# Mamba-2 scan and cosine router on one core: sums of weights, a data-dependent loop and its tables moved in the order of the work

## The chip, the cores and the metric

The kernel runs on one NeuronCore of a Trainium2 chip. The metric is the time in microseconds (us) that the device takes for one launch; the time before is 300.6 us, the median of three runs (297.8 to 301.43). The core has five engines that each work through a queue of their own, in order: TensorE (PE: matmuls; PEld is its weight load), VectorE (DVE), ScalarE (ACT), GpSimd (POOL) and SyncE (SP, which here only starts DMAs). They meet through semaphores. Matmuls read from the on-chip memory SBUF and write sums to another, PSUM.

## The reference

A Mamba-2 scan makes 3072 tokens of 256 features, and a router with 8 experts turns each token into its output:

```
for c in range(nc):                               # scan in chunks
    y[:, :, sl] = (CB * L) @ xc + (Cc @ state) * exp(cum)
    state = decay_full * state + sum_j B_j x_j * decay_from_j
x = y.transpose(0, 2, 1, 3).reshape(3072, 256)
logits = normed(x) @ normed(expert_emb).T / tau
expert_idx = argmax(logits); gate = softmax(logits)[expert_idx]
for e in range(8):
    mask = expert_idx == e
    out[mask] = gate[mask, None] * (relu(x[mask] @ w1[e]) @ w2[e])
```

w1 is 8 x 256 x 1024, w2 is 8 x 1024 x 256, all in float32.

## The kernel before, in words

**The scan** (`mamba`) computes the tokens chunk by chunk, finds each token's expert, and scatters each token's row into a table `rows` in DRAM, sorted by expert. It ends at about 97 us of the profiled execution. **The experts** (`moe`) then run over that table. Room is made for 416 tokens of each expert (4 tiles of 104). What an expert has beyond that, "leftover" tokens, would be computed by a loop whose length is only known when the kernel runs; with these inputs its length is zero, and the loop's body is skipped by a branch.

The work is a list `parts` of ten, run in order:

- parts 0 and 1: the early **halves** (2 tiles) of experts 0 and 1, whose tokens come from the first chunks; part 0's upward product is still in the scan, its downward product opens the experts;
- parts 2 and 3: the late halves of experts 0 and 1;
- parts 4 to 9: the **whole experts** 2 to 7 (4 tiles each), of the class `Seven`.

A half (class `Job`) is an upward product `up` (eight groups of hidden features, L745, the relu alternately on ACT and on DVE), then `turn_x` (transposes of the next part's tokens on PE, L723), `turn_copies`, `prepare` (DVE, L703 to L714: it makes the rows to write to, `to`, and each token's `gate`; its square root is a `pow` on POOL, L696, and its exponential is on ACT, L710), and a downward product `down` (L762), whose two results ACT and DVE copy to `yoT` (L767, L769). The finished tokens of a part are turned, scaled and written during the next part's `up`, in `out`: transposes on PE (L778), a scaling `yo` on DVE or ACT in turn (L781, L783; four buffers), then on POOL a memset of `tick` (L784) and an indirect DMA (L785).

A whole expert uses Strassen-like products with seven instead of eight block products. It needs sums of weights, which POOL makes ahead of time: `mix_up` makes `m1` from w1 and `mix_down` makes `m2` from w2, four instructions each (L806, 128 x 512 float32). Each of `m1` and `m2` has two buffers. It also needs differences of the tokens, `dx`, four subtractions on DVE (`mix_x`, L825) at the end of the part ahead of it.

**The order.** Nothing is scheduled by a planner: `manual_schedule` keeps each engine's queue in the order in which the program issues instructions. The helper `part(i)` issues part i and then what prepares the parts after it. In the kernel before, the sums for part 4 are issued at the start of part 2 (`mix_up`) and of part 3 (`mix_down`), the sums for part i + 2 are issued at the end of part i from part 3 on, and behind a whole expert's products stands a copy of one number of its `gate` to `tick` on POOL (L965), ahead of the sums: POOL waits there until DVE has finished that part's `prepare`. Parts 1 to 3 have no such copy.

`leftover_blocks` (L1004 to L1059) computes the loop's tables in 23 small DVE instructions; it is issued at the end of part 1. `leftover` (L1062) stands between parts 7 and 8. It loads the number of blocks into a register of every engine (L1066) and branches on it (L1067). Where the body is skipped, each engine raises the semaphores by what the body would have raised; on POOL that includes the semaphores of its indirect DMAs (INC_SWDGE_SEM).

DMAs on SP: `begin(i + 3)` loads the tokens `xg` of a later part (two buffers), `load_weights` the weights of an expert (three buffers).

Of the kernel before, what the change touches and what calls it, by code (L numbers as in the profile page):

```python
# [28 lines left out]
EE, EC, HT = 2, 4, 2  # L29
# [173 lines left out]
def load_weights(k, e):  # L203
    k.w1t[e] = k.wp.tile([128, KD, F], F32, name="w1", tag="w1")
    k.nc.sync.dma_start(k.w1t[e][:], k.w1[e].rearrange("(k p) f -> p k f", p=128))
    k.w2t[e] = k.wp.tile([128, KF, DM], F32, name="w2", tag="w2")
    k.nc.sync.dma_start(k.w2t[e][:], k.w2[e].rearrange("(f p) m -> p f m", p=128))
# [721 lines left out]
def moe(k):  # L929
    parts = [(j, k.early_has[:TR, e, :]) for e, j in enumerate(k.early)]  # L930
    for e in range(EE):
        parts.append((Job(k, HT, TR, k.w1t[e], k.w2t[e]), k.late_has[:TR, e, :]))
    n = E + EE

    def begin(i):
        e = i - EE
        if e < EE:
            parts[i][0].load(k.p.tile([TR, HT, W], F32, name="xg", tag="xg"), T * e + HT * TR)
        else:
            parts.append((Seven(k, NT, TR, k.w1t[e], k.w2t[e]), k.has[:TR, e - EE, :]))  # L940
            parts[i][0].load(k.p.tile([TR, NT, W], F32, name="xg", tag="xg"), T * e)

    def part(i):
        j, has = parts[i]
        last, new = parts[i - 1][0], parts[i + 1][0] if i + 1 < n else None
        new_seven = isinstance(new, Seven)

        def out(at):
            if 0 <= at and 2 * at < last.nt:
                last.out(2 * at, 2)  # L950

        def turn():
            if new:
                new.turn_copies(k.nc.scalar.copy if new_seven else None)
            if new_seven:
                new.mix_x()

        if isinstance(j, Seven):
            for f in range(KF // 2):
                j.up(f)  # L960
                out(f)
            j.up(KF // 2, new.turn_x if new else None)
            j.mix_h()
            j.down(turn, lambda: j.prepare(has))
            k.nc.gpsimd.tensor_copy(out=k.tick[:], in_=j.gate[0:1, 0:1])  # L965
        else:
            if i == EE:
                parts[2 * EE][0].mix_up()
            elif new_seven:
                new.mix_down()  # L970
            for f in range(KF):
                j.up(f)
                out(f - 1)
                if f == 3:
                    j.measure()
            new.turn_x()
            turn()
            j.prepare(has)
            j.down(0, j.nt)
        if 2 * EE < i + 2 < n:  # L980
            parts[i + 2][0].mix_up()
            parts[i + 2][0].mix_down()
        if i == 1:
            leftover_blocks(k)
        if 0 <= i - EE < E - 3:
            load_weights(k, i - EE + 3)
        if i + 3 < n:
            begin(i + 3)

    with k.tc.manual_schedule():  # L990
        begin(EE)
        begin(EE + 1)
        parts[1][0].turn_x()
        parts[1][0].turn_copies()
        parts[0][0].down(0, HT)
        for i in range(1, n - 2):
            part(i)
        leftover(k)
        for i in range(n - 2, n):
            part(i)  # L1000
        parts[n - 1][0].out(0, NT)


def leftover_blocks(k):  # L1004


    nc = k.nc

    def tile_(name, shape, dtype=F32):
        return k.p.tile(shape, dtype, name=name, bufs=1)  # L1010

    def tt(out, in0, in1, op):
        nc.vector.tensor_tensor(out=out, in0=in0, in1=in1, op=op)


    over = tile_("over", [128, E])
    nc.vector.tensor_scalar(
        out=over[:], in0=k.n[:], scalar1=float(CAP), scalar2=0.0, op0=ALU.subtract, op1=ALU.max
    )
    n_i = tile_("n_i", [128, E], I32)  # L1020
    nc.vector.tensor_scalar(out=n_i[:], in0=over[:], scalar1=float(Q - 1), scalar2=None, op0=ALU.add)
    nc.vector.tensor_single_scalar(n_i[:], n_i[:], 7, op=ALU.arith_shift_right)
    nb = tile_("nb", [128, E])
    nc.vector.tensor_copy(out=nb[:], in_=n_i[:])
    zero = tile_("zero", [128, E])
    nc.vector.memset(zero[:], 0.0)
    end = tile_("end", [128, E])
    nc.vector.tensor_tensor_scan(out=end[:], data0=nb[:], data1=zero[:], initial=0.0, op0=ALU.add, op1=ALU.add)
    begin = tile_("begin", [128, E])
    tt(begin[:], end[:], nb[:], ALU.subtract)  # L1030


    be = [128, LEFT, E]
    mine, tmp = tile_("mine", be), tile_("mine_not", be)
    step = k.step[:].unsqueeze(2).to_broadcast(be)
    tt(mine[:], begin[:].unsqueeze(1).to_broadcast(be), step, ALU.is_le)
    tt(tmp[:], end[:].unsqueeze(1).to_broadcast(be), step, ALU.is_le)
    tt(mine[:], mine[:], tmp[:], ALU.subtract)

    def of(name, v):  # L1040
        r = tile_(name, [128, LEFT])
        tt(tmp[:], mine[:], v.unsqueeze(1).to_broadcast(be), ALU.mult)
        nc.vector.reduce_sum(out=r[:], in_=tmp[:], axis=AX.X)
        return r

    ef = of("left_e", k.step[:, 0:E])
    bf = of("left_b", begin[:])
    nf = of("left_n", over[:])
    tt(bf[:], k.step[:], bf[:], ALU.subtract)
    nc.vector.tensor_scalar_mul(bf[:], bf[:], float(Q))  # L1050
    tt(nf[:], nf[:], bf[:], ALU.subtract)
    rf = tile_("left_r", [128, LEFT])
    nc.vector.tensor_scalar(out=rf[:], in0=ef[:], scalar1=float(T), scalar2=float(CAP), op0=ALU.mult, op1=ALU.add)
    tt(rf[:], rf[:], bf[:], ALU.add)
    table = tile_("table", [128, 2, LEFT], I32)
    nc.vector.tensor_copy(out=table[:, 0, :], in_=ef[:])
    nc.vector.tensor_copy(out=table[:, 1, 0:1], in_=end[:, E - 1 : E])

    k.left = table, rf, nf  # L1059


def leftover(k):  # L1062
    nc = k.nc
    table, rf, nf = k.left
    SP = mybir.EngineType.SP
    blocks = nc.values_load(table[0:1, 1, 0:1], min_val=0, max_val=LEFT)  # L1066
    with k.tc.If(blocks > 0):  # L1067
        with k.tc.For_i(0, blocks, 1) as i:
            e = nc.values_load(table[0:1, 0, bass.ds(i, 1)], engines=(SP,), min_val=0, max_val=E - 1)
            w1 = k.wp.tile([128, KD, F], F32, name="w1", tag="w1")  # L1070
            nc.sync.dma_start(w1[:], k.w1[bass.ds(e, 1)].rearrange("o (k p) f -> p (o k) f", p=128))
            w2 = k.wp.tile([128, KF, DM], F32, name="w2", tag="w2")
            nc.sync.dma_start(w2[:], k.w2[bass.ds(e, 1)].rearrange("o (f p) m -> p (o f) m", p=128))
            j = Job(k, 1, Q, w1, w2)
            has = k.p.tile([128, 1], I32, name="left_has", tag="left_has")
            nc.vector.tensor_tensor(out=has[:], in0=k.part[:], in1=nf[:, bass.ds(i, 1)], op=ALU.is_lt)
            r = k.p.tile([128, 1], F32, name="left_p", tag="left_p")
            nc.vector.tensor_tensor(out=r[:], in0=k.part[:], in1=rf[:, bass.ds(i, 1)], op=ALU.add)
            at_f = k.p.tile([128, 1], F32, name="left_atf", tag="left_atf")
            nc.vector.memset(at_f[:], float(E * T))  # L1080
            nc.vector.copy_predicated(at_f[:], has[:], r[:])
            at = k.p.tile([128, 1], I32, name="left_at", tag="left_at")
            nc.vector.tensor_copy(out=at[:], in_=at_f[:])
            x = k.p.tile([128, 1, W], F32, name="left_x", tag="left_x")
            nc.vector.memset(x[:], 1.0)
            j.gather(x, at)
            j.turn_x()
            j.turn_copies()
            j.measure()
            j.prepare(has[:])  # L1090
            for f in range(KF):
                j.up(f)
            j.down(0, 1)
            j.out(0, 1)
# [3 lines left out]
def kernel(  # L1098
# [35 lines left out]
    with (  # L1134
        tc.tile_pool(name="moe", bufs=2, reuse_waits="tile") as p,
        tc.tile_pool(name="moe_ps", bufs=1, space=PSUM, reuse_waits="tile") as ps,
    ):
        k.p, k.ps = p, ps
        moe(k)
# [43 lines left out]
```

## Time and profile before

| what | value |
|---|---|
| median of three runs | 300.6 us |
| profiled execution, its own time | 300.56 us |
| its span, first to last instruction | 298.8 us |
| mean granted TensorE clock | 0.967 of full |
| busy: PE, DVE, POOL, ACT | 259.4, 196.4, 155.7, 101.1 us |
| sums of weights on POOL (L806) | 48 instructions, 61.4 us |

The span runs from the first to the last instruction of the core; the 1.8 us beyond it lie around the program. Times in the profile count from the span's start. The granted clock is the share of full speed (2.4 GHz) that TensorE's clock was given; it has two levels, 1.2 and 2.4 GHz, so a mean between them is a stretch that was partly at the lower one. A row of a timeline says when an instruction (or several alike) began, how long it took, and in square brackets how long its engine had been idle before, and for what.

### The profile page before, as it was taken

The page shows a single profiled execution, that of the slowest core. Times are in us where ns is not written, and L with a number is a line of the kernel's source. Part 1 is how long each engine was busy: PE and PEld are TensorE (multiplying, and loading weights), DVE is VectorE, ACT ScalarE, POOL GpSimd, SP SyncE. Part 2 cuts the span into 40 slices and gives each one's busy share as a digit, 9 for nine tenths or more (in the row PEclk, how much of TensorE's full clock was granted, in tenths as well). Part 3 has the DMA queues.
Part 4 walks back from the last instruction along what each step waited for, and adds up shares of the span by engine and source line. Part 5 has one row for each costly group of instructions (what it writes and reads, how often), then busy time and mean ns, then how long its engine had stood idle before and what let it go on. Part 6 is the DMA issues. An engine that isn't in the chain of part 4 may idle for free.

```text
span 298.8 us, 5806 instructions
## 1 busy us (share of the span) xinstructions
PE 259.4 (87%) x2084; PEld 236.0 (79%) x2084; DVE 196.4 (66%) x558; ACT 101.1 (34%) x306; POOL 155.7 (52%) x226
## 2 busy tenths in 40 slices
PE   0888999999877999799599999999999876999960
PEld 0665788887755999799499999999999866998950
DVE  7577888998423168866857768768768544766830
ACT  2312534442333123032134354354255223524420
POOL 8015456774356081659620398397497495105132
PEclk9999999999999999799779999999999997999995
DMA  5987399922221210183550281371361201001001
GB/s 174 361 304 288 130 331 322 400 77 78 72 102 55 82 29 0 31 264 106 147 216 0 62 283 39 94 264 47 97 253 52 65 0 40 12 1 56 2 17 40
DMA packets 18232, 37.30 MB, mean 125 GB/s; under 512 B 2042, under 2 KB 10439, under 8 KB 18202
## 3 DMA queue, kind: packets, MB, share of 16 engines
q1 hardware_dynamic: 15338, 30.36, 30.1%
q0 software_dynamic: 2688, 6.50, 6.7%
q8 instruction: 17, 0.28, 0.4%
q14 instruction: 13, 0.11, 0.1%
q10 hardware_dynamic: 176, 0.06, 0.1%
HBM read 26.80 MB, written 10.37 MB: 124 GB/s over the span
## 4 chain that ended last, share of the span: by engine, by line
PE 51%; DVE 17%; DMA 17%; POOL 5%; issue 5%; ACT 3%; ACTq 1%; POOLq 0%; DVEq 0%
PE sum L829 23%; DMA out_dram<-yo,to 15%; PE sum L762 6%; PE sum L745 5%; DVE g L321 4%; PE pg L315 3%; POOL m L806 3%; PE pg L745 3%; DVE dx L825 2%; PE pf L250 2%; PE pz L369 2%; POOL out_dram L785 2%; PE turned L723 1%; PE py L351 1%; DMA xe<-rows 1%
## 5 line engine op out<-in xcount | busy, mean ns | idle before, releaser
L785 POOL DMA_INDIRECT out_dram<-yo,to x32 | 34.4, 1075 | 35.0 <-DVE yo L781 19.9
L829 PE MATMUL sum<-dx,m 128*128 128x208 f32 x144 | 36.2, 363 | 7.8 <-DVE part L837 4.5
L837 DVE TENSOR_TENSOR part<-sum,part 128x208 f32<-128x208 f32 x60 | 22.2, 371 | 31.6 <-ACT part L842 20.6
L595 POOL DMA_INDIRECT rows<-yt,row_of x24 | 23.8, 990 | 24.0 <-issue 11.3
L829 PEld LDWEIGHTS sum<-dx,m 128*128 128x128 f32 x144 | 26.4, 199 | 11.0 <-DVE part L837 6.8
L321 DVE TENSOR_TENSOR g<-pg,mask 128x1024 f32<-128x1024 f32 x24 | 28.2, 1217 | 5.6 <-PE pg L315 5.5
L806 POOL TENSOR_TENSOR m<-w 128x512 f32<-128x512 f32 x24 | 30.7, 1280 | 0.0
L837 DVE TENSOR_TENSOR h<-sum,part 128x208 f32<-128x208 f32 x72 | 25.1, 370 | 7.9 <-PE sum L829 5.4
L696 POOL TENSOR_TENSOR gr<-gr,half 104x4 f32<-104x4 f32 (+1 forms) x10 | 9.3, 929 | 34.3 <-ACT sq L692 34.3
L829 PE MATMUL sum<-dh,m 128*128 128x208 f32 x144 | 26.7, 342 | 0.5
L829 PEld LDWEIGHTS sum<-dh,m 128*128 128x128 f32 x144 | 25.0, 190 | 2.3 <-issue 2.3
L829 PE MATMUL sum<-xT,w 128*128 128x208 f32 x96 | 25.2, 358 | 1.0 <-DVEq L1067 1.0
L762 PE MATMUL sum<-hT,w 128*128 128x208 f32 x128 | 24.1, 348 | 0.0
L762 PEld LDWEIGHTS sum<-hT,w 128*128 128x128 f32 x128 | 23.2, 197 | 0.0
L745 PE MATMUL sum<-xT,w 128*128 128x208 f32 x96 | 18.7, 347 | 1.9 <-DVE hT L751 1.9
L315 PE MATMUL pg<-cm,bt 32*128 32x256 f32 x192 | 19.5, 439 | 0.3 <-DVE g L321 0.3
L842 ACT COPY part<-sum 128x208 f32<-128x208 f32 x36 | 11.9, 330 | 20.9 <-PE sum L829 20.9
L829 PEld LDWEIGHTS sum<-xT,w 128*128 128x128 f32 x96 | 17.9, 202 | 1.4 <-issue 1.3
L829 PE MATMUL sum<-h,w 128*128 128x208 f32 x96 | 18.8, 339 | 0.0
L745 PEld LDWEIGHTS sum<-xT,w 128*128 128x128 f32 x96 | 17.0, 193 | 2.2 <-DVE hT L751 2.2
L260 ACT ACTIVATE cm<-cp,tmask 128x256 f32<-128x256 f32 x24 | 10.9, 500 | 21.0 <-DVE cp L255 21.0
L882 ACT ACTIVATE h<-h 128x208 f32<-128x208 f32 x24 | 9.1, 377 | 24.9 <-DVE h L837 24.9
(209 smaller groups left out, 551.7 us busy)
## 6 DMA issues: line engine op xcount, KB each, us to landing
w<-in_moe_w_dram SPq DMA_DIRECT2D x16, 1024.0 KB
rows<-none SPq DMA_DIRECT2D x8, 442.0 KB
x<-in_x_dram SPq DMA_DIRECT2D x6, 512.0 KB
xg<-rows SPq DMA_DIRECT2D x6, 442.0 KB
b<-in_B_dram SPq DMA_DIRECT2D x6, 256.0 KB
ct<-in_CT_dram SPq DMA_DIRECT2D x6, 256.0 KB
out_dram<-yo,to POOLq DMA_INDIRECT x32, 2.6
xe<-rows SPq DMA_DIRECT2D x2, 221.0 KB
```

Of the source, the lines that this page charges most:

```text
L260: nc.scalar.activation(s.cm[:, :, v, :], s.cp[:], ACT.Copy, scale=k.tmask[:, v : v + 1])
L315: nc.tensor.matmul(k.pg[:, q, 256 * i : 256 * i + 256], lhsT=s.bt[r, i, :], rhs=s.cm[r, i], start=True, stop=True, tile_position=(32 * q, 0),)
L321: nc.vector.tensor_tensor(out=g[:], in0=k.pg[:, :, 256 * i : 256 * i + 256].rearrange("p q (t i) -> p q t i", t=2), in1=k.mask[:].unsqueez ...
L595: d = nc.gpsimd.indirect_dma_start(out=k.rows[:, :], out_offset=bass.IndirectOffsetOnAxis(ap=k.to[g][:, u : u + 1], axis=0), in_=k.yt[:, N ...
L696: nc.gpsimd.tensor_tensor(out=s.r[:], in0=s.r[:], in1=k.half[0:tr, 0:nt], op=ALU.pow)
L745: nc.tensor.matmul(t, lhsT=s.w1[:, j, 128 * f : 128 * f + 128], rhs=s.xT[:, j, :], start=(j == 0), stop=(j == KD - 1))
L762: nc.tensor.matmul(t, lhsT=s.w2[:, f, 128 * j : 128 * j + 128], rhs=s.hT[:, f, c], start=(f == 0), stop=(f == KF - 1),)
L785: d = nc.gpsimd.indirect_dma_start(out=k.out[:, :], out_offset=bass.IndirectOffsetOnAxis(ap=s.to[:, i : i + 1], axis=0), in_=y[:], in_offs ...
L806: s.k.nc.gpsimd.tensor_tensor(out=out, in0=in0, in1=in1, op=op)
L829: s.k.nc.tensor.matmul(ps, lhsT=lhsT(i, g), rhs=rhs(j, g), start=(first and g == gs[0]), stop=(g == gs[-1]), skip_group_check=True,)
L837: s.k.nc.vector.tensor_tensor(out=out, in0=in0, in1=in1, op=ALU.add)
L842: s.k.nc.scalar.copy(out=out, in_=ps)
```

## The change

Three things are moved, and one is added. The tables of the loop (`leftover_blocks`) are issued right behind the scan, ahead of part 0's `down`, and no longer at the end of part 1. The loop (`leftover`) moves into `part(7)`, ahead of the copy to `tick` and of the sums for part 9; both stood ahead of it. The sums of part 4 are issued at the end of part 1 (`mix_up`) and of part 2 (`mix_down`), no longer at the start of parts 2 and 3. And the copy of `gate` to `tick` on POOL now stands behind every part, the halves too, ahead of the sums that follow. The sums for part i + 2 come behind `load_weights` and `begin`, which go to another queue.

```diff
             j.down(turn, lambda: j.prepare(has))
-            k.nc.gpsimd.tensor_copy(out=k.tick[:], in_=j.gate[0:1, 0:1])
         else:
-            if i == EE:
-                parts[2 * EE][0].mix_up()
-            elif new_seven:
-                new.mix_down()
             for f in range(KF):
...
             j.down(0, j.nt)
-        if 2 * EE < i + 2 < n:
-            parts[i + 2][0].mix_up()
-            parts[i + 2][0].mix_down()
-        if i == 1:
-            leftover_blocks(k)
         if 0 <= i - EE < E - 3:
             load_weights(k, i - EE + 3)
         if i + 3 < n:
             begin(i + 3)
+        if i == n - 3:
+            leftover(k)
+
+
+        k.nc.gpsimd.tensor_copy(out=k.tick[:], in_=j.gate[0:1, 0:1])
+        if i == EE - 1:
+            parts[2 * EE][0].mix_up()
+        elif i == EE:
+            parts[2 * EE][0].mix_down()
+        elif i + 2 < n:
+            parts[i + 2][0].mix_up()
+            parts[i + 2][0].mix_down()

     with k.tc.manual_schedule():
         begin(EE)
         begin(EE + 1)
         parts[1][0].turn_x()
         parts[1][0].turn_copies()
+        leftover_blocks(k)
         parts[0][0].down(0, HT)
-        for i in range(1, n - 2):
-            part(i)
-        leftover(k)
-        for i in range(n - 2, n):
+        for i in range(1, n):
             part(i)
         parts[n - 1][0].out(0, NT)
```

## Rows read from the trace of the kernel before

**Rows 1.** The page's chain that ended last, as shares of the span.

```profile
PE 51%; DVE 17%; DMA 17%; POOL 5%; issue 5%; ACT 3%; ACTq 1%; POOLq 0%; DVEq 0%
```

**Rows 2.** Windows of 5 us: busy PE, PEld, DVE, ACT, POOL; clock, DMA.

```profile
120.00:125.00 5.00, 3.85 (x16) 3.67 (x17) 3.80 (x17) 0.34 (x1) 2.96 (x5) 0.72 0.14 34
...
235.00:240.00 5.00, 3.98 (x25) 3.64 (x24) 2.67 (x10) 0.71 (x3) 3.69 (x4) 1.00 0.35 94
```

**Rows 3.** Timeline of PE in the halves: start, duration, line, idle before.

```profile
96.73 5.81 PE L762 MATMUL sum<-hT,w 128*128 128x208 f32 x32
...
108.80 5.81 PE L762 MATMUL sum<-hT,w 128*128 128x208 f32 x32
...
121.15 2.20 PE L745 MATMUL sum<-xT,w 128*128 128x208 f32 x8 [1.88 <-DVE hT L751]
...
137.12 5.81 PE L762 MATMUL sum<-hT,w 128*128 128x208 f32 x32
```

**Rows 4.** Timeline of DVE in the halves.

```profile
102.58 0.38 DVE L769 COPY yoT<-sum 128x208 f32<-128x208 f32 x1 [5.11 <-PE sum L762]
...
114.94 0.16 DVE L1017 TENSOR_SCALAR over<-n 128x8 f32<-128x8 f32 x1
...
120.67 0.15 DVE L1057 CAST table<-end 128x1 int32<-128x1 f32 x1
```

**Rows 5.** The chain in order of time: start, duration, what.

```profile
103.95 0.44 PE turned L778 x4
```

**Rows 6.** Timeline of POOL: sums of weights, pow, copy to tick.

```profile
108.13 1.30 POOL L806 TENSOR_TENSOR m<-w 128x512 f32<-128x512 f32 x1
...
136.13 1.27 POOL L806 TENSOR_TENSOR m<-w 128x512 f32<-128x512 f32 x1
...
231.49 1.05 POOL L696 TENSOR_TENSOR gr<-gr,half 104x4 f32<-104x4 f32 x1 [1.16 <-ACT sq L692]
236.23 0.18 POOL L965 COPY tick<-gate 1x1 f32<-1x1 f32 x1 [3.69 <-DVE gate L714]
```

**Rows 7.** Instructions of line 806: shortest, median, longest in ns, first and last start.

```profile
L806 POOL TENSOR_TENSOR m<-w x24: 1252/1268/1404, 108.1 to 244.0; 128x512 f32<-128x512 f32 x24
```

**Rows 8.** Timeline of DVE ahead of parts 4 and 8.

```profile
137.50 2.83 DVE L825 TENSOR_TENSOR dx<-xT 128x208 f32<-128x208 f32 x2 [0.52 <-ACT xT L731]
...
145.73 0.92 DVE L709 TENSOR_TENSOR gl<-gl,gr 104x16 f32<-104x16 f32 x1
...
232.93 0.65 DVE L825 TENSOR_TENSOR dx<-xT 128x208 f32<-128x208 f32 x2
```

**Rows 9.** Timeline of PE in parts 4, 5 and 8.

```profile
142.77 0.52 PE L829 MATMUL sum<-xT,w 128*128 128x208 f32 x2
...
147.26 1.03 PE L829 MATMUL sum<-dx,m 128*128 128x208 f32 x2 [3.27 <-ACT yoT L767]
...
158.77 0.88 PE L723 MATMUL turned<-ident,xg 104*128 104x104 f32 x8
...
170.38 0.52 PE L829 MATMUL sum<-xT,w 128*128 128x208 f32 x2
...
180.72 0.88 PE L723 MATMUL turned<-ident,xg 104*128 104x104 f32 x8
...
237.43 0.59 PE L829 MATMUL sum<-xT,w 128*128 128x208 f32 x2 [1.02 <-DVEq L1067]
...
248.94 1.06 PE L829 MATMUL sum<-dx,m 128*128 128x208 f32 x2 [4.27 <-DVE part L837]
...
253.63 0.88 PE L723 MATMUL turned<-ident,xg 104*128 104x104 f32 x8
```

**Rows 10.** Timeline of ACT in part 8.

```profile
247.78 0.47 ACT L783 ACTIVATE yo<-turned,gate 104x256 f32<-104x256 f32 x1 [4.37 <-DMA out_dram<-yo,to]
```

**Rows 11.** Instructions of line 1067: durations in ns, first and last start.

```profile
L1067 POOLq INC_SWDGE_SEM  x1: 1069/1069/1069, 246.7 to 246.7; - x1
```

**Rows 12.** The page's costliest groups: busy us, mean ns, idle before.

```profile
L785 POOL DMA_INDIRECT out_dram<-yo,to x32 | 34.4, 1075 | 35.0 <-DVE yo L781 19.9 <-DVE hT L751 8.6 <-issue 4.3
```

## The prediction, made before the changed kernel had run

> **What bounds the kernel now.** I read the chain by engine first, then the clock by windows, then PE's timeline, and last the queues that PE waits for. The chain gives PE about half of the span [rows 1]. Its share of DMA looks like a second bound but is none: it hangs on the output writes, and no output is read again, except through a buffer that has to come free. So PE's timeline decides, and what counts there are its gaps and the stretches in which it runs at the lower clock. Behind the scan three gaps stand out, and each has a slow stretch behind it.
>
> Gap A: in part 1, PE idles 1.88 us for a relu on DVE [rows 3]. DVE is then computing the loop's tables, one after the other from 114.94 to 120.82 [rows 4]. In the window from 120 to 125 the granted clock is 0.72, so PE ran partly at 1.2 instead of 2.4 GHz [rows 2].
>
> Gap B: where part 4 begins, PE idles 3.27 us, for ACT's copy of part 3's result [rows 9]. ACT works in order, and ahead of that copy is the exponential of `prepare`, which waits for `gl` on DVE, finished only at 146.65 [rows 8]. DVE is late because its subtractions run beside POOL's sums: two of `dx` take 2.83 us there, and 0.65 us ahead of part 8, with POOL idle [rows 8]. The sums that do it are those for part 5, started at 136.13 [rows 6], and not those of part 4.
>
> Gap C: in part 8, PE idles 4.27 us for DVE, which waits for ACT's `part`, which stands behind a `yo` that waited 4.37 us for an output DMA [rows 9, 10]. No such DMA was under way: the skipped loop would have written one, and POOL makes up for it with INC_SWDGE_SEM. That starts at 246.7 and takes 1.07 us [rows 11], so it ends at 247.8, which is when `yo` starts. It was late because POOL first did the eight sums for part 9.
>
> **The change part by part.** The sum is made against the profiled execution's 300.56 us; the median of the runs is 300.6, so nothing is converted.
>
> *Tables.* They move into a hole: DVE idles 5.11 us ahead of its copy of part 0's result, from 97.47 to 102.58 [rows 4]. The tables take 120.82 - 114.94 = 5.88 us, so they end at about 103.35, and the copy (0.38) at 103.73 instead of 102.96. Who waits for that copy? The transposes of part 0's output, at 103.95 [rows 5]; the next relu on DVE isn't before that either. Two tenths remain. I cost the new place at nothing: part 0's `down` on PE covers it, and if the cover is gone each late tenth is one of PE's. What the old place cost comes from a comparison. From one `down` to the next PE needs 108.80 - 96.73 = 12.07 undisturbed; over the next two halves it takes 137.12 - 108.80 = 28.32 [rows 3]. Two halves make 24.14, and four more transposes ahead of the last one 0.44 (four others cost that [rows 5]). A is 28.32 - 24.14 - 0.44 = **3.74**: the gap, and 1.86 of slow clock.
>
> *Copies to `tick` in the halves.* Three copies of 0.18 on POOL [rows 6]; POOL is not PE's bound there. What they change is when the sums run. For part 4 the new issue place alone moves nothing: POOL's queue held these sums between the same neighbours before. With the copy, `mix_up` starts when part 1's gate is done, some 3 to 4 us later than the 108.13 of before [rows 6], and `mix_down` likewise; part 4 is far off. Queued behind the waiting copy are the sums, then two output DMAs of 1.08 us [rows 12], then the `pow` that the next gate needs: 0.18 + 4 x 1.27 + 2.2 + at most 1.05 = 8.5 us [rows 6, 7, 12], and from a first `dx` to a finished gate 236.23 - 232.93 = 3.3 us at most [rows 6, 8]. Together 11.8, within the 12.07 of a half. So it is hidden.
>
> The copy behind part 3 is what pays. The sums for part 5 start only when `dx` and `prepare` are through: estimated at 137.50 - 3.74 + 3.3 = 137.1, while part 4 begins on PE at 142.77 - 3.74 = 139.0. That is how parts 5 to 7 already run. SP's queue keeps its order; its loads wait for readers in parts 2 and 3 and move ahead with these, so the weights of part 5 are no later against its sums than before.
>
> B is then read by comparing part 4 with part 5, from the first product to the transposes of the next tokens: 158.77 - 142.77 = 16.00 against 180.72 - 170.38 = 10.34 [rows 9]. Part 5 writes four tiles there and part 4 two, four transposes or 0.44 less, so 9.90 would be right. B is **6.10**: the gap, and 2.83 of slow clock.
>
> *The loop ahead of the sums.* POOL has been idle since its `pow` ended at 232.54 and waits for the gate until 236.23 [rows 6]. In this hole it now loads the register, branches and raises the semaphores (1.07 [rows 11]). They are up some ten microseconds ahead of the `yo` that wants them. Part 9's sums start no later as long as the branch costs POOL under 3.7 us; if more, they have until part 9. On the other engines the loop keeps its place, so the gap of 1.02 us in which PE waits for DVE at the branch [rows 9] stays. C, in the same stretch of part 8: 253.63 - 237.43 = 16.20, less 10.34, is **5.86** [rows 9]: the gap, and 1.59 of slow clock.
>
> **The sum:** 300.56 - 3.74 - 6.10 - 5.86 = **284.9 us**. What is late next is that gap of 1.02 us and the end of the kernel, where four outputs leave one after the other; neither is touched.
>
> **The clock, row and rule.** Gaps of 1.88 us and more were followed by slow stretches; the one of 1.02 was not: its window shows a granted clock of 1.00 [rows 2]. I take the slow stretches as going with their gaps. The Trainium skill ("TensorE: Matmul & The Clock Gate", Part 1) says that the watch on TensorE's activity runs freely and does not start with the kernel, so that the same program shows a different number of slow matmuls from run to run. By that, a gap that went unpunished can be punished once everything ahead of it has moved; this is the first rival below.
>
> **The rivals.**
>
> 1. *The gap that stays costs the clock.* Place: the branch behind part 7. For it: three of four gaps were followed by slow matmuls [rows 2, 9]. Against: it is the shortest. Price: the slow stretch of the nearest gap, 1.86, so 286.7.
> 2. *The tables collide.* Place: DVE behind the scan. For it: only two tenths of room. Against: DVE idles there, and POOL, which slows it elsewhere, has nothing to add up then. Price: from nothing to all of A, up to 288.6.
> 3. *C comes back.* POOL's increment waits for something late in its new place too, or ACT's `yo` was held by a real output. Against: it started the moment the increment ended [rows 10, 11]. Price 5.86: 290.7.
> 4. *The change doesn't do what it says for B:* sums still meet `dx`, because `prepare` is late for a cause that the trace doesn't show. Price up to 6.10: 291.0.
> 5. *Slower: POOL becomes the bound of the halves.* With the copies, gate, sums, outputs, `pow` and the next gate form a loop of at most 11.8 us. It decides once it exceeds 12.07. The sums run between 1.25 and 1.40 each even against `dx` [rows 7], and at 1.40 throughout the bound is only 0.3 over. But DVE's `dx` grew by a factor of 4.3 [rows 8]; if POOL's sums paid that factor in their new place, a half would need 11.8 + 3.3 x 5.08 = 28.6, two halves 33 us more: about 318.
>
> **How the numbers follow.** Forecast 0.70, rivals 1 to 5: 0.10, 0.08, 0.06, 0.04, 0.02. Low end: the gap of 1.02 disappears as well (283.9), less 1.1 for the scatter of the runs shown: 282.8. High end: rival 2 in full, 288.6, and a little scatter: 288.8. That leaves out rivals 3 to 5. About 2% is what a measurement of this kernel tells from no change; faster by that means under 294.6. One of A, B or C failing alone still lies under it; only B and C failing together (0.03, out of rivals 3 and 4) would end within 2%. So faster 0.95, same 0.03, slower 0.02.
>
> **What would show it.** PE starts `down` of part 3 at about 133.4 instead of 137.12, with 12.07 between the `down`s; part 4 begins near 139.0 and reaches its transposes 9.9 us later; `dx` ahead of part 4 takes 0.65 for two; the sums for part 5 start behind the gate, near 137; INC_SWDGE_SEM runs ahead of part 9's sums, and part 8 reaches its transposes 10.3 us after its first product. Wrong it would be by an idle PE at 104, by a `pow` in parts 2 or 3 that comes after DVE wants it, or by slow matmuls in part 8.

## The result, and the profile after

The changed kernel takes 284.9 us, the median of 4 runs (284.4 to 285.2), against 300.7 (297.8 to 301.4, 4 runs) for the kernel before on the same chip: a ratio of 0.949 [0.943, 0.956]. In a later comparison on another chip it was 284.7 (284.1 to 285.0, 6 runs) against 299.4, a ratio of 0.951 [0.947, 0.954], a gain of 14.8 us. The medians of the kernel before lay between 298.8 and 300.7 over five comparisons. One of the runs below, at 286.7 us with both edits at the branch, was in a slower state and is left out. The profiled execution of the changed kernel took 285.2 us, its span is 283.5.

The timeline of PE in the changed kernel, at the places of [rows 3] and [rows 9]:

```profile
97.22 5.81 PE L762 MATMUL sum<-hT,w 128*128 128x208 f32 x32
...
109.29 5.81 PE L762 MATMUL sum<-hT,w 128*128 128x208 f32 x32
...
121.36 5.81 PE L762 MATMUL sum<-hT,w 128*128 128x208 f32 x32
...
133.79 5.81 PE L762 MATMUL sum<-hT,w 128*128 128x208 f32 x32
...
139.44 0.52 PE L829 MATMUL sum<-xT,w 128*128 128x208 f32 x2
...
149.47 0.88 PE L723 MATMUL turned<-ident,xg 104*128 104x104 f32 x8
...
228.17 0.59 PE L829 MATMUL sum<-xT,w 128*128 128x208 f32 x2 [1.02 <-DVEq L1067]
...
238.60 0.88 PE L723 MATMUL turned<-ident,xg 104*128 104x104 f32 x8
```

The three gaps of A, B and C are gone, and the account closes by stretches:

| stretch of PE | before | after | saved | forecast |
|---|---|---|---|---|
| `down` of part 1 to `down` of part 3 (A) | 28.32 | 24.50 | 3.82 | 3.74 |
| part 4, first product to transposes (B) | 16.00 | 10.03 | 5.97 | 6.10 |
| part 8, first product to transposes (C) | 16.20 | 10.43 | 5.77 | 5.86 |
| span to the first `down` (the scan) | 96.73 | 97.22 | -0.49 | 0 |

The three stretches make 15.56, and the span fell by 15.3, from 298.8 to 283.5: the scan, which nothing in the change touches, took 0.49 more, and 0.2 were saved elsewhere. The gap of 1.02 at the branch is still there.

DVE in the changed kernel (timeline): the tables from 97.87 to 103.76, the copy they push back, the `gr` of part 2 that needs POOL's `pow`, and the two `dx` ahead of part 4.

```profile
97.87 0.16 DVE L1017 TENSOR_SCALAR over<-n 128x8 f32<-128x8 f32 x1
...
103.61 0.15 DVE L1057 CAST table<-end 128x1 int32<-128x1 f32 x1
103.67 0.36 DVE L769 COPY yoT<-sum 128x208 f32<-128x208 f32 x1
...
122.47 0.16 DVE L707 TENSOR_SCALAR gr<-gr 104x2 f32<-104x2 f32 x1
...
134.18 0.78 DVE L825 TENSOR_TENSOR dx<-xT 128x208 f32<-128x208 f32 x2 [0.52 <-ACT xT L731]
```

The two `dx` take 0.78 where they took 2.83 [rows 8]. POOL's timeline shows why: the sums for part 5 now stand behind a copy to `tick` that waits 4.68 us for the gate.

```profile
120.02 0.75 POOL L696 TENSOR_TENSOR gr<-gr,half 104x2 f32<-104x2 f32 x1
...
137.53 0.18 POOL L983 COPY tick<-gate 1x1 f32<-1x1 f32 x1 [4.68 <-DVE gate L714]
137.68 1.26 POOL L806 TENSOR_TENSOR m<-w 128x512 f32<-128x512 f32 x1
...
226.98 0.18 POOL L983 COPY tick<-gate 1x1 f32<-1x1 f32 x1 [3.70 <-DVE gate L714]
```

The increment of line 1067 (durations in ns, first and last start) lies in the hole ahead of the last of these copies:

```profile
L1067 POOLq INC_SWDGE_SEM  x1: 1069/1069/1069, 223.5 to 223.5; - x1
```

And the window (columns as in [rows 2]) that had a clock of 0.72 shows 1.00 now. So does part 8, from 228 to 239, behind the gap that stayed.

```profile
120.00:125.00 5.00, 5.00 (x32) 4.96 (x31) 2.37 (x13) 0.89 (x3) 1.74 (x4) 1.00 0.38 91
```

### The profile page after: what moved, and what is told of

It reads as the page before. It is cut to its first block, busy times and chain, and to the rows that moved or that the text cites. A ratio compares the mean times of both kernels' runs of the same rounds, so it can differ in the third digit from the quotient of the medians.

```text
span 283.5 us, 5813 instructions
## 1 busy us (share of the span) xinstructions
PE 254.3 (90%) x2084; PEld 232.0 (82%) x2084; DVE 182.5 (64%) x558; ACT 101.3 (36%) x306; POOL 156.2 (55%) x229
## 5 line engine op out<-in xcount | busy, mean ns | idle before, releaser
L837 DVE TENSOR_TENSOR part<-sum,part 128x208 f32<-128x208 f32 x60 | 22.3, 371 | 25.7 <-ACT part L842 19.3
L829 PE MATMUL sum<-dx,m 128*128 128x208 f32 x144 | 34.3, 350 | 0.0
L837 DVE TENSOR_TENSOR h<-sum,part 128x208 f32<-128x208 f32 x72 | 25.0, 370 | 7.0 <-PE sum L829 4.4
L829 PEld LDWEIGHTS sum<-dx,m 128*128 128x128 f32 x144 | 24.9, 189 | 3.1 <-DVE part L837 2.5
L829 PE MATMUL sum<-xT,w 128*128 128x208 f32 x96 | 23.7, 340 | 1.0 <-DVEq L1067 1.0
L762 PE MATMUL sum<-hT,w 128*128 128x208 f32 x128 | 23.2, 340 | 0.0
L762 PEld LDWEIGHTS sum<-hT,w 128*128 128x128 f32 x128 | 22.3, 190 | 0.0
L983 POOL COPY tick<-gate 1x1 f32<-1x1 f32 x9 | 1.6, 178 | 32.2 <-DVE gate L714 32.2
L745 PE MATMUL sum<-xT,w 128*128 128x208 f32 x96 | 17.9, 339 | 0.0
L829 PEld LDWEIGHTS sum<-xT,w 128*128 128x128 f32 x96 | 16.7, 190 | 1.3 <-issue 1.3
```

The source lines that it names most:

```text
L745: nc.tensor.matmul(t, lhsT=s.w1[:, j, 128 * f : 128 * f + 128], rhs=s.xT[:, j, :], start=(j == 0), stop=(j == KD - 1))
L762: nc.tensor.matmul(t, lhsT=s.w2[:, f, 128 * j : 128 * j + 128], rhs=s.hT[:, f, c], start=(f == 0), stop=(f == KF - 1),)
L829: s.k.nc.tensor.matmul(ps, lhsT=lhsT(i, g), rhs=rhs(j, g), start=(first and g == gs[0]), stop=(g == gs[-1]), skip_group_check=True,)
L837: s.k.nc.vector.tensor_tensor(out=out, in0=in0, in1=in1, op=ALU.add)
```

## The experiments

The first five take moves of the change back, one alone, two together or a part of one, and leave the rest. Their ratios to the kernel before are set against the 0.951 of the changed kernel's six runs, and a hundredth of the ratio is 3 us.

**Tables back behind part 1.**

```diff
+        if i == 1:
+            leftover_blocks(k)
...
-        leftover_blocks(k)
         parts[0][0].down(0, HT)
```

> The changed kernel with the loop's tables back at the end of part 1, all else as changed. Theory (each gap has its own price and they add): only gap A returns, 284.9 + 3.7 = 288.6 us, with PE idle for about 1.9 us near 119 to 121 and the lower clock behind it. Rival (the slow clock is not tied to its gap): only the gap returns, 1.9, so 286.8. Rival (the tables cost nothing where they were, once the sums no longer slow DVE): 284.9.

Measured: 291.0 us (290.4 to 293.6), ratio 0.970 [0.965, 0.976]. About 6 us came back, not 3.7. PE's timeline shows a gap of 3.30 where [rows 3] has 1.88, and the two halves take 141.81 - 111.01 = 30.80, so 6.30 more than in the changed kernel. The granted clock is 0.50 from 124 to 130 us, behind the gap:

```profile
111.01 5.81 PE L762 MATMUL sum<-hT,w 128*128 128x208 f32 x32
...
124.78 3.14 PE L745 MATMUL sum<-xT,w 128*128 128x208 f32 x8 [3.30 <-DVE hT L751]
...
141.81 5.81 PE L762 MATMUL sum<-hT,w 128*128 128x208 f32 x32
```

The gap grew by 1.42 because two of the first table operations on DVE took 0.53 and 1.22, where they had taken 0.16 and 0.17:

```profile
117.15 0.53 DVE L1018 TENSOR_SCALAR over<-n 128x8 f32<-128x8 f32 x1
117.71 1.22 DVE L1022 TENSOR_SCALAR n_i<-over 128x8 int32<-128x8 f32 x1
```

POOL's sums for part 4, which the new copies delay, were running at that moment:

```profile
117.60 1.28 POOL L806 TENSOR_TENSOR m<-w,m 128x512 f32<-128x512 f32 x1
```

So the old place had become worse by another part of the same change. That is a reading of one trace; the next kernel tests it.

**Tables back, and no copies behind parts 1 and 2**, which puts the sums for part 4 early again:

```diff
+        if i == 1:
+            leftover_blocks(k)
...
-        k.nc.gpsimd.tensor_copy(out=k.tick[:], in_=j.gate[0:1, 0:1])
+        if i > 2:
+            k.nc.gpsimd.tensor_copy(out=k.tick[:], in_=j.gate[0:1, 0:1])
...
-        leftover_blocks(k)
         parts[0][0].down(0, HT)
```

> The changed kernel with the loop's tables back at the end of part 1 and without the copies behind parts 1 and 2, so that the sums of part 4 run early again. Theory (the extra 2.4 us of putting the tables back came from these late sums slowing two table instructions and from a longer gap with a longer slow stretch): 284.9 + 3.8 = 288.7 us, a gap near 1.9 instead of 3.3, the first two table instructions near 0.17 each instead of 0.53 and 1.22. Rival (the copies have nothing to do with it): 291.0 again.

Measured: 288.4 us (287.6 to 288.7), ratio 0.966 [0.959, 0.972]. The table operations are at 0.16 and 0.17 again and the gap at 1.89, so the collision was with these sums. PE's timeline:

```profile
109.41 5.81 PE L762 MATMUL sum<-hT,w 128*128 128x208 f32 x32
...
121.77 1.67 PE L745 MATMUL sum<-xT,w 128*128 128x208 f32 x8 [1.89 <-DVE hT L751]
...
123.64 5.81 PE L762 MATMUL sum<-hT,w 128*128 128x208 f32 x32
...
131.16 0.54 PE L778 MATMUL turned<-ident,yoT 128*104 128x128 f32 x3 [0.19 <-DVE yoT L769]
...
136.47 5.81 PE L762 MATMUL sum<-hT,w 128*128 128x208 f32 x32
```

But the two halves take 27.06, only 2.56 more than the changed kernel's 24.50, where the kernel before took 3.82 more. The gap is the same; the slow clock behind it is missing. The granted clock is 1.00 in every microsecond from 119 to 132, and the `down` behind the gap takes 5.81, as the undisturbed ones do. In the kernel before, the clock was 0.50 from 123 to 125, and this `down` (PE's timeline) took longer:

```profile
123.84 6.67 PE L762 MATMUL sum<-hT,w 128*128 128x208 f32 x32
```

Of the 2.56, 1.89 are the gap, and 0.39 come from a second wait, the 0.19 in the fence: the four transposes take 131.53 - 130.70 = 0.83 with it, and 0.44 without. DVE's copy to `yoT` is late there, behind a `prepare` that ran beside POOL's `pow` and sums (its predicated copy took 2.35). The rest lies at the edges of the two gaps.

**The old tables stay out, but no copies behind parts 1 and 2**, to see what these two copies are worth alone:

```diff
-        k.nc.gpsimd.tensor_copy(out=k.tick[:], in_=j.gate[0:1, 0:1])
+        if i > 2:
+            k.nc.gpsimd.tensor_copy(out=k.tick[:], in_=j.gate[0:1, 0:1])
```

> The changed kernel without the copies behind parts 1 and 2 alone; the one behind part 3 stays. Theory (only the copy behind part 3 pays, since the sums of part 4 slow DVE in parts 1 and 2 with room to spare): 284.9 us, within 0.5, though prepare in parts 1 and 2 takes 2 to 3 us longer on DVE. Rival (the copies in parts 1 and 2 also keep PE from a gap): above 286.

Measured: 285.1 us (285.0 to 285.5), ratio 0.951 [0.946, 0.956]: the two copies are worth nothing with the tables in their new place. They aren't idle for all that. Without them POOL's sums for part 4 meet `prepare` on DVE (timeline of DVE):

```profile
110.39 1.16 DVE L704 COPY_PREDICATED to_f<-early_has,xe 104x2 f32<-104x2 int32 x1
111.58 1.19 DVE L706 CAST to<-to_f 104x2 int32<-104x2 f32 x1
```

With the copies such operations take 0.16 and 0.17. In the halves of this kernel nothing on PE waits for them (the stretch of A takes 24.51), so it costs no time. The sums at that moment, on POOL:

```profile
110.26 1.27 POOL L806 TENSOR_TENSOR m<-m,w 128x512 f32<-128x512 f32 x1
111.48 1.27 POOL L806 TENSOR_TENSOR m<-w 128x512 f32<-128x512 f32 x1
```

**No copies in the halves at all**, the one behind part 3 included:

```diff
+        if i > 3:
+            k.nc.gpsimd.tensor_copy(out=k.tick[:], in_=j.gate[0:1, 0:1])
```

> The changed kernel without the copies of gate to tick behind parts 1, 2 and 3; the sums of part 4 stay at their new places. Theory (the copy is what pays in B, the new issue place of part 4's sums moves nothing): all of B returns, 284.9 + 6.1 = 291.0 us, two dx take near 2.8 us again, and PE idles over 3 us where part 4 begins. Rival (the new place of part 4's sums pays): near 284.9.

Measured: 290.3 us (288.8 to 291.0), ratio 0.967 [0.961, 0.973], so 5 us came back. The sums for part 5 start at 132.49 again, ahead of `dx`, and part 4 on PE has its old gap and takes 155.17 - 139.13 = 16.04:

```profile
139.13 0.52 PE L829 MATMUL sum<-xT,w 128*128 128x208 f32 x2
...
143.63 1.03 PE L829 MATMUL sum<-dx,m 128*128 128x208 f32 x2 [3.28 <-ACT yoT L767]
...
155.17 0.88 PE L723 MATMUL turned<-ident,xg 104*128 104x104 f32 x8
```

With the experiment before it: of the three new copies, the one behind part 3 carries all of B. The sums of part 4 kept their new issue places here; no run takes that move back by itself, but the kernel with one copy alone, below, has B gone with these sums in their old places.

**The loop behind the sums again**, in `part(7)`:

```diff
-        if i == n - 3:
-            leftover(k)
...
             parts[i + 2][0].mix_up()
             parts[i + 2][0].mix_down()
+        if i == n - 3:
+            leftover(k)
```

> The changed kernel with the loop's branch behind the sums for part 9 again, all else as changed. Theory (POOL's increment of its DMA semaphores behind the sums holds ACT's yo): gap C returns, 284.9 + 5.9 = 290.8 us, the increment ends when yo starts. Rival (yo was held by a real output, which the other two edits have moved ahead): 284.9.

Measured: 291.8 us (291.1 to 292.0), ratio 0.973 [0.968, 0.979], so 6.8 us came back. The increment starts at 237.1, ends at 238.2, and ACT's `yo` starts at 238.19 after 4.38 us of waiting, as in [rows 10, 11]. On PE the gap is the old one, the stretch is not: 245.10 - 227.83 = 17.27, which is 6.84 over the changed kernel's 10.43 and 1.07 over [rows 9].

```profile
227.83 0.59 PE L829 MATMUL sum<-xT,w 128*128 128x208 f32 x2 [1.02 <-DVEq L1067]
...
239.35 1.06 PE L829 MATMUL sum<-dx,m 128*128 128x208 f32 x2 [4.28 <-DVE part L837]
...
245.10 0.88 PE L723 MATMUL turned<-ident,xg 104*128 104x104 f32 x8
```

Undone one by one, the parts give back 6.0, 4.9 and 6.8 us, 17.7 together where the whole change gained 14.8. Two causes of the difference show: the collision of the tables (291.0 against 288.4, or 1.5 us by the two ratios) and the longer slow stretch of C (6.84 against 5.86). The next two kernels make one move each on the kernel before.

**The copy behind part 3 alone**, on the kernel before:

```diff
+        if i == 3:
+            k.nc.gpsimd.tensor_copy(out=k.tick[:], in_=j.gate[0:1, 0:1])
         if 2 * EE < i + 2 < n:
```

> The kernel before with one edit: a copy of gate to tick behind part 3, ahead of the sums for part 5. Theory (that copy alone makes B): 6.0 us less than before on the same chip, a ratio of 0.980, two dx near 0.7 to 0.8 us. Rival (B also needs the sums of part 4 elsewhere, or the time of the first gap): less than 3 us gained, a ratio over 0.990.

Measured: 294.8 us (293.6 to 295.4), ratio 0.987 [0.980, 0.994]: 4.0 us, neither the 6 of the theory nor the under 3 of the rival. In the profile B is gone in full (part 4 takes 10.03, the two `dx` 0.78). The other two gaps, whose causes were left as they were, are the same to 0.01, but they cost something else than before:

```profile
109.17 5.81 PE L762 MATMUL sum<-hT,w 128*128 128x208 f32 x32
...
121.53 1.67 PE L745 MATMUL sum<-xT,w 128*128 128x208 f32 x8 [1.89 <-DVE hT L751]
...
136.22 5.81 PE L762 MATMUL sum<-hT,w 128*128 128x208 f32 x32
...
242.09 1.06 PE L829 MATMUL sum<-dx,m 128*128 128x208 f32 x2 [4.26 <-DVE part L837]
...
247.82 0.88 PE L723 MATMUL turned<-ident,xg 104*128 104x104 f32 x8
```

A takes 27.05, which is 1.27 less than in [rows 3], ahead of anything that the copy changes: the granted clock stays at 1.00 behind this gap too. C takes 247.82 - 230.59 = 17.23, 1.03 more than in [rows 9]. The two nearly cancel, so they don't explain the 4.0: the profiled run, 294.75, lies 5.8 below the profiled run of before (300.56). The 4.0 is counted from a median of 298.9, which is 1.7 below that run. Where those runs were shorter was not profiled; an A without slow clock would make most of it.

**The tables alone**, on the kernel before:

```diff
-        if i == 1:
-            leftover_blocks(k)
...
+        leftover_blocks(k)
         parts[0][0].down(0, HT)
```

> The kernel before with one edit: the loop's tables behind the scan. Theory (A is 3.7 to 3.8 on its own, and the 6.1 that came back when only the tables were put back holds a collision with the sums of part 4, which the copies had made later): 3.8 us less than before, a ratio of 0.987, 12.07 between the downs. Rival (A is worth 6 by itself): a ratio of 0.980.

Measured: 296.3 us (295.2 to 298.1, 10 runs), ratio 0.993 [0.990, 0.996]: 2.1 us (2.5 by the medians), not 3.8. In its profile A is gone (132.78 - 108.28 = 24.50), B costs 6.13 and C 5.82, all as the sum has them. So the move does what was forecast. That it gains less would follow if in most runs of the kernel before A costs the 2.55 of two of the other kernels, without slow clock, and not the 3.8 of the profile on which the sum was made; those runs were not profiled, so this is argued and not shown.

**Tables made longer**, by four operations of 0.42 us on DVE, in the changed kernel:

```diff
     nf = of("left_n", over[:])
+    for _ in range(4):
+        tt(tmp[:], mine[:], over[:].unsqueeze(1).to_broadcast(be), ALU.mult)
```

> The changed kernel with four more instructions of 0.42 us in the tables behind the scan, 1.7 us longer in all; their result is not used. Theory (two tenths of room, then each tenth is one of PE's): PE idles 1.3 to 1.5 us at the transposes near 104. If the clock keeps full speed behind it, as behind the gap of 1.02, 286.3 us; if it falls, as behind the gap of 1.88, about 288.2. Rival (PE is covered by more than the two tenths): 284.9.

Measured: 286.6 us (284.8 to 288.3), ratio 0.958 [0.950, 0.966]. The transposes of part 0's output wait, and the next `down` is late by 112.44 - 98.89 - 12.07 = 1.48 us:

```profile
98.89 5.81 PE L762 MATMUL sum<-hT,w 128*128 128x208 f32 x32
...
107.48 0.54 PE L778 MATMUL turned<-ident,yoT 128*104 128x128 f32 x3 [1.26 <-DVE yoT L769]
...
112.44 5.81 PE L762 MATMUL sum<-hT,w 128*128 128x208 f32 x32
```

DVE's copy to `yoT` starts 107.06 - 98.89 = 8.17 us behind the first `down` here and 103.67 - 97.22 = 6.45 in the changed kernel. Of these 1.72 us, 1.48 reach PE, so 0.24 was free: the "two tenths" of the prediction, and each late tenth beyond them is one of PE's. No slow stretch follows this gap of 1.26: the next `down`s are 12.07 apart again.

**The gap of 1.02 at the branch.** Two edits try to take it away, each alone and then together: the loop's sums in another buffer, so that DVE's branch has nothing to pass on to PE, and the number of blocks loaded at the end of part 1.

```diff
             j = Job(k, 1, Q, w1, w2)
+            j.sum = j.turned
```

> The changed kernel; in the loop that is skipped, the sums use the PSUM buffers of the transposes instead of those of the sums, so that PE's first product behind the branch no longer depends on what DVE would have released in the loop. Theory (the gap of 1.02 us that stays is PE waiting for DVE to reach the branch): the gap falls below 0.3, 284.9 - 0.8 = 284.1 us. Rival (PE waits at the branch for itself, or the wait moves to the first transposes): unchanged, 284.9.

```diff
+        if i == 1:
+            k.blocks_left = k.nc.values_load(k.left[0][0:1, 1, 0:1], min_val=0, max_val=LEFT)
...
-    blocks = nc.values_load(table[0:1, 1, 0:1], min_val=0, max_val=LEFT)
+    blocks = k.blocks_left
```

> The changed kernel with the loads of the number of blocks into the engines' registers moved from the branch to the end of part 1; the branch stays. Theory (half of the gap of 1.02 us is DVE's register load of 0.54 us): the gap falls to about 0.5, 284.4 us, if the five early loads of 0.5 us stay covered. Rival (an early load costs PE or DVE as much there): unchanged or slower, up to 285.5.

Measured in one comparison: the first edit 284.5 us (283.3 to 286.3), ratio 0.948 [0.945, 0.951], the second 284.1 (283.6 to 284.7), ratio 0.947 [0.945, 0.950]. The gap falls to 0.30 and to 0.57. In a second comparison both edits together, beside the changed kernel once more:

> The changed kernel with both edits at the branch: the early register load and the skipped loop's sums in the other PSUM buffers. Theory (PE then waits at the branch only for itself, 0.3 us as in the run with the loop's sums elsewhere, or less): gap 0.2 to 0.3 us, part 8's transposes within 10.5 us of its first product, 0.7 us less than the changed kernel on the same chip, about 284.1; that is under the spread that the scan's slow matmuls make (up to 2 us), so the trace decides and not the median. Rival (the early loads cost PE something at the end of part 1): the downs stand further apart than 12.07.

> The changed kernel once more, beside the one with both edits at the branch. Theory: 284.9 us within 0.5 by the median, a gap of 1.02 us at the branch and full speed behind it. Rival (the gap that stays costs the clock in some executions): single runs up to 2 us slower and, in the profiled one, part 8's transposes over 11 us behind its first product.

Both together take 283.9 us (282.4 to 285.0, 5 runs), ratio 0.951 [0.947, 0.955]; the changed kernel 284.7, ratio 0.951 [0.947, 0.954]. By the times the two can't be told apart. PE's timeline with both edits:

```profile
225.34 0.59 PE L829 MATMUL sum<-xT,w 128*128 128x208 f32 x2 [0.30 <-PEq L1069]
```

From the first `down`, at 95.09, to part 8 it needs 130.25 us, and the changed kernel's second profile 227.81 - 96.84 = 130.97: the 0.72 by which the gap fell are saved in the trace. The times don't resolve that: the scan alone differs by up to 4.0 us between the profiles, and the runs of both edits spread over 2.6 us. I would keep the edits for the trace's sake; no time here shows them to be faster.

## Why the prediction came out

**The mechanisms** held, each shown by undoing it. The tables delayed a relu, and in their new place they have 0.24 us of room. The sums for part 5 made B by meeting `dx`, and the copy behind part 3 alone removes it. The increment held ACT's `yo`, and does so again when the loop stands behind the sums. The marks stood where they were put: `down` of part 3 at 133.79 for 133.4, part 4 at 139.44 for 139.0, the sums for part 5 at 137.68 for 137.1; each is later by about the 0.49 that the scan took more.

**The costs taken at nothing.** POOL did not become the bound of the halves: part 2's `pow` ended at 120.77 and DVE wanted it at 122.47, 1.7 us later. The sums ran in 1.25 to 1.28 each.

**The rivals.** The first, that the gap of 1.02 costs the clock, did not come in either profile of the changed kernel: the stretch of part 8 behind it took 10.43 and 10.44, where part 5 of [rows 9] took 10.34. In the nine other profiles with that gap no slow stretch follows it directly either. The other rivals did not come.

**The step whose size was off** is the price of A: "the gap, and 1.86 of slow clock". The gap is real and the same each time (1.88 to 1.89). But the slow clock followed it in the profile of before alone; in two later profiles with the same gap the granted clock stayed at 1.00, A cost 2.55 and 2.56 (the gap, a second wait of about 0.4 and edges) and not 3.82, and the tables alone gained 2.1 us. "I take the slow stretches as going with their gaps" is therefore wrong for A, and as a price it is wrong for all three, since the profile shows one draw. For C the draw was a low one: about 1.5 there and with the tables alone, about 2.5 in two other kernels. For B it was the same each time (5.97 to 6.13 for all of B in three profiles). That the sum 3.74 + 6.10 + 5.86 met the time so closely is partly luck: a high and a low draw stood side by side, and the profiled execution (300.56) was near the upper end of the medians of before (298.8 to 300.7). With 2.5 for A, 6.0 for B and 5.8 to 6.8 for C the gain is 14.3 to 15.3, and the more precise of the two comparisons has 14.8.

Three small terms were off or unsupported. The four more transposes in A, set at 0.44, took 24.50 - 24.14 = 0.36. Part 4 without B took 10.03, not 9.90. And the 1.1 us of scatter at the low end of the range follows from no row: the three runs of before reached from 2.8 under their median to 0.8 above it.

**Still open:** what decides whether a gap is followed by slow matmuls, and for how long. No run here tells.

## What to carry to other kernels

Price an idle gap of PE as two terms: the gap, which repeated to 0.02 here, and the slow matmuls behind it, of which one profile shows one draw; give the second a range from zero up, and do not add up single moves to the tenth. When DVE is late on small operations, look at what POOL does at that moment: a copy of one element that makes POOL wait for the gate was worth 4 to 6 us. And a loop that is skipped still has a price on every queue: put it where POOL idles, and look who waits for the semaphores that it raises.

## What the runs showed of the hardware

**A gap with and without slow matmuls behind it.** The clearest case is the scan, which no kernel here changes. In the kernel before (PE's timeline) there is a gap of 1.20, and the eight products of line 369 behind it take 1.19:

```profile
27.93 0.20 PE L187 MATMUL pz<-ident,emb 8*128 8x8 f32 x1 [1.20 <-DVE emb L181]
...
29.44 1.19 PE L369 MATMUL pz<-turn,yT 128*128 128x136 f32 x8
```

In the changed kernel the gap is 1.39, the first products behind it are as quick (0.20), and then the eight take 2.04:

```profile
27.94 0.20 PE L187 MATMUL pz<-ident,emb 8*128 8x8 f32 x1 [1.39 <-DVE emb L181]
...
29.45 2.04 PE L369 MATMUL pz<-turn,yT 128*128 128x136 f32 x8
```

By then the granted clock (a window, columns as in [rows 2]) has fallen to 0.50:

```profile
30.00:32.00 2.00, 2.00 (x17) 1.67 (x20) 1.81 (x4) 0.68 (x2) 2.00 (x5) 0.50 0.09 34
```

A third case looks alike and is another. In the kernel with the loop's sums elsewhere the gap is 1.19 and the eight take 2.18, but PE was slow ahead of the gap already: three products of line 315 take 0.80 ahead of it and 0.80 behind it, and in the kernel before 0.80 and 0.48. Here no clock fell; it had not risen yet.

```profile
21.51 0.80 PE L315 MATMUL pg<-cm,bt 32*128 32x256 f32 x3
...
27.94 0.24 PE L187 MATMUL pz<-ident,emb 8*128 8x8 f32 x1 [1.19 <-DVE emb L181]
...
28.53 0.80 PE L315 MATMUL pg<-cm,bt 32*128 32x256 f32 x3
...
30.79 2.18 PE L369 MATMUL pz<-turn,yT 128*128 128x136 f32 x8
```

Over all 14 profiles that gap is 1.19 to 2.09 long. In five (gaps of 1.20 to 1.58) the eight products took 1.19. In six (gaps of 1.38 to 2.09) the clock had risen and fell again behind the gap, and they took 1.65 to 2.18. In three (gaps of 1.19) it had not risen. The first `down` starts at 96.2 to 96.9 in the first five, at 97.1 to 97.5 in five of the six, and at 98.9 to 99.1 in the three. The sixth, with both edits, has it at 95.1: there the clock first rose earlier, since the eight products of line 146 at 19 us take 1.04, and 1.86 in the changed kernel's second profile. That is as much as the runs of one kernel spread (up to 4 us); which of the cases an unprofiled run had is not known. The Trainium skill ("TensorE: Matmul & The Clock Gate", Part 1) says that the watch on TensorE's activity runs freely, so that the same program has a different number of slow matmuls from run to run; these rows agree, though they don't show the watch.

**A granted clock of 1.00 beside slow matmuls.** The window of that third kernel in which the eight products took 2.18 shows a clock of 1.00 all the same:

```profile
30.00:32.00 2.00, 2.00 (x12) 1.35 (x7) 1.81 (x4) 0.59 (x2) 2.00 (x4) 1.00 0.01 5
```

Its trace holds no record of the clock ahead of 34.95 us, and the column reads 1.00 where there is none, ahead of the first rise in every profile here. In such a stretch the durations told more than the column.

**Some operations of DVE wait until POOL's instruction is over.** In the kernel without copies behind parts 1 and 2, the predicated copy ends at 110.39 + 1.16 = 111.55 and POOL's sum at 110.26 + 1.27 = 111.53; the cast behind it ends at 112.77, POOL's next sum at 112.75. With the tables back, the slow one ends at 118.93 and the sum at 118.88. So operations on 2 or 8 columns, 0.17 us long by themselves, took as long as POOL's instruction had left. Not all do: in the same kernel the reciprocal at 112.88 took its 0.17 inside POOL's sum of 112.71 to 113.98, and in the changed kernel the adds with one input in PSUM (L837) took their 0.36 to 0.38 beside the sums for part 5. I had priced this for `dx`, with its 208 columns, alone. The Trainium skill ("SBUF — State Buffer", Who interferes with whom) says that DVE, in its two-port modes or with two inputs in SBUF, and GpSimd lock a pair of ports that they share for a whole instruction, and that the other blocks fully; other operations of DVE don't contend. These ends, 0.02 to 0.05 us apart, and the adds agree.
